# Splitting half of a weight matrix one group earlier, beside the first layer

## The chip, the cores and the metric

One core of a Trainium2 chip (trn2). The metric is device time of one execution, in microseconds (us). A ratio is the mean time of one kernel's fast runs over that of the other kernel's fast runs of the same rounds on the same chip, with a 95% interval, so it is not quite the ratio of the medians quoted beside it.

## The reference, cut to what matters

An attention with a decaying state (batch 4, 8 heads, 768 positions, width 48) gives a matrix x of 3072 rows and 384 columns. Four experts then work on all rows:

```python
p = domain_probs / (domain_probs.sum(-1, keepdims=True) + 1e-09)
for e in range(4):
    h = np.maximum(x @ w1[e], 0.0)          # w1[e]: 384 x 1024
    out += p[:, e:e + 1] * (h @ w2[e])      # w2[e]: 1024 x 384
```

Everything is float32, and the result has to be exact to that precision.

## The kernel before

The 3072 rows are 24 units of 128, in groups of 2, 4, 4, 4, 4, 4 and 2. For each group and expert the kernel runs the first layer (eight hidden tiles, each 128 hidden values by up to 512 rows), then the second layer (for each unit eight products of 128 x 128 by 128 x 384, one per hidden tile). Pieces of the next group's attention are put between the products.

An exact product is made in one of two ways. Either both operands are whole fp32, or both are three rounded parts (top, low and dif, type fp32r), and the product is top x top plus low x low in one sum and dif x dif in a second sum. (dif is made of top and low, so dif x dif holds both mixed terms, top x low and low x top. The first sum is scaled by 1 + 1/4096, FINE, and what dif x dif has too much then cancels. So three products do the work of four.) Making the parts of a weight piece takes two passes on ScalarE and two on VectorE. Each piece is split once, used and stored to memory ("kept", 1152 KB), and later groups load it from there.

```python
split1 = lambda gi, e: gi > 0        # first layer in parts from the second group (gi = 1) on
split2 = lambda gi, e: gi > 1        # second layer in parts from the third group on
makes  = [lambda gi, e: gi == 0, lambda gi, e: gi == 1]   # where w1 and w2 are split
```

So in the second group w2 is loaded whole, used whole, and split beside the second layer. The weights are loaded when the first layer begins (pieces 0 and 1) and at its third tile (2 and 3), into the parts of the hidden tiles that whole hidden values do not use:

```python
def up(gi, e, fc, slots=None):                       # one hidden tile of the first layer
    # ... [cut]
    if fc in ((0, 2) if gi == 1 else (0,)) and begins and not split2(gi, e):
        for k in half: load_piece(1, (gi * E + e) * NQ + k, beside=True)
    # ... [cut: nine matmuls into "one" (6) and "two" (3)]
        nc.scalar.activation(out=t, in_=one, func=ACT.Copy, scale=FINE)
        if split2(gi, e):
            nc.vector.tensor_add(t, t, two)
            finish.append(hidden_parts(t, parts))    # ScalarE: top; VectorE: low, dif (two halves)
        else:
            nc.vector.tensor_add(whole, t, two)
            finish.append(rectified(whole))          # ScalarE alone

def split_piece(l, i):
    whole = wt[l][i]
    # ... [cut]
    nc.scalar.activation(out=top, in_=whole, func=ACT.Copy, scale=TRIM)
    yield
    nc.scalar.activation(out=dif, in_=whole, func=ACT.Copy, scale=TRIM * 4096)
    yield
    nc.vector.scalar_tensor_tensor(out=low, in0=whole, scalar=4096.0, in1=dif.bitcast(F32), ...)
    nc.vector.tensor_sub(dif, low.bitcast(F32), top.bitcast(F32))
    nc.gpsimd.dma_start(out=kept[l][i % (E * NQ)], in_=w.bitcast(F32))

def down(gi, e, slots, between):                     # second layer: slots = one unit, or two in parts
    if slots[0] == 0 and makes[1](gi, e):
        making.extend(split_piece(1, first + k) for k in range(NQ))      # NQ = 4 pieces
    # ... [cut]
    steps = [(part, i, fc) for parts, tiles in (kinds if halves_ else [((3,), range(FCH))])
             for part in parts for i in range(len(slots)) for fc in tiles]   # part 3: whole
    # ... [cut: one matmul per step, then add_up() of each finished sum on VectorE]
    # after the last units of an expert: next group's pieces
        for c in range(NQ):
            if c < NQ // 2 or gi == LAST: load_piece(1, first + NQ + c)
            else: late.append(first + NQ + c)        # loaded after a later w1 piece
```

## Time and profile before

The time is 1080.85 us, the median of 3 runs (1079.32 to 1081.3). The prediction below shows the profile lines that carry the argument. What matters of them and of the starts of each layer in the timeline of TensorE (PE) is this; a stretch runs from the first matmul of one layer to the first of the next:

| | before |
|---|---|
| PE busy in the whole span | 98% |
| second group: length, PE idle in it | 185.54, 0.39 us |
| second group, experts 0 to 3: first layer | 21.66, 21.22, 22.22, 22.14 us |
| second group, experts 0 to 3: second layer | 27.03, 24.38, 23.40, 23.48 us |
| third group, expert 0: first, second layer | 22.64, 19.43 us |

Read it from the last row up. The same second layer takes 19.4 us where both operands are in parts and 23.4 to 24.4 us where they are whole (27.0 for expert 0, between whose products more of the attention lies). PE hardly idles in either. So most of the difference is work of the products, and it can be saved wherever the parts are ready in time.

### The profile page before, as it was taken

The page shows a single profiled execution, that of the slowest core. Times are in us where ns is not written, and L with a number is a line of the kernel's source. Part 1 is how long each engine was busy: PE and PEld are TensorE (multiplying, and loading weights), DVE is VectorE, ACT ScalarE, POOL GpSimd, SP SyncE. Part 2 cuts the span into 40 slices and gives each one's busy share as a digit, 9 for nine tenths or more (in the row PEclk, how much of TensorE's full clock was granted, in tenths as well). Part 3 has the DMA queues.
Part 4 walks back from the last instruction along what each step waited for, and adds up shares of the span by engine and source line. Part 5 has one row for each costly group of instructions (what it writes and reads, how often), then busy time and mean ns, then how long its engine had stood idle before and what let it go on. Part 6 is the DMA issues. An engine that isn't in the chain of part 4 may idle for free.

```text
span 1079.8 us, 21595 instructions
## 1 busy us (share of the span) xinstructions
PE 1055.5 (98%) x8460; PEld 899.6 (83%) x8460; DVE 774.5 (72%) x1711; ACT 566.8 (52%) x1202; POOL 32.7 (3%) x71
## 2 busy tenths in 40 slices
PE   8889899999999999999999999999999999999998
PEld 8767677676777798898898998888989889898988
DVE  5588678656557878777877786986878866666565
ACT  5786766764747455536446445555564543323232
POOL 2000000000000100000000000000000000000000
PEclk9999899999999999999999999999999999999999
DMA  8597679886686968659568568595594643544440
GB/s 124 155 329 227 213 230 378 301 315 240 234 295 208 399 203 318 253 147 351 204 221 324 195 228 320 159 327 222 168 352 146 249 191 136 215 172 180 182 182 33
DMA packets 158838, 251.67 MB, mean 233 GB/s; under 512 B 120112, under 2 KB 135344, under 8 KB 136208
## 3 DMA queue, kind: packets, MB, share of 16 engines
q1 hardware_dynamic: 149600, 208.82, 56.2%
q0 software_dynamic: 5760, 41.29, 9.7%
q8 instruction: 67, 1.10, 0.4%
q10 hardware_dynamic: 3376, 0.17, 0.3%
q14 instruction: 35, 0.29, 0.1%
HBM read 207.79 MB, written 42.47 MB: 232 GB/s over the span
## 4 chain that ended last, share of the span: by engine, by line
PE 80%; DVE 8%; ACT 6%; issue 2%; SPq 2%; DMA 1%; ACTq 0%; DVEq 0%
PE ops L615 26%; PE one L531 21%; PE two L531 10%; PE ops L619 9%; PE sc L333 5%; PE yps L425 3%; PE tp L265 2%; ACT qb L307 2%; PE one L523 2%; PE sps L454 1%; DVE near L343 1%; DVE hT L571 1%; PE far L388 1%; DVE t L544 1%; SPq L211 1%
## 5 line engine op out<-in xcount | busy, mean ns | idle before, releaser
L615 PE MATMUL ops<-w,hT 128*128 128x384 f32 x1728 | 318.6, 340 | 2.8 <-DVE acc L649 2.8
L615 PEld LDWEIGHTS ops<-w,hT 128*128 128x128 f32 x1728 | 299.1, 188 | 8.2 <-DVE acc L649 4.1
L531 PE MATMUL one<-xT,w 128*128 128x512 f32 x960 | 253.7, 400 | 0.8 <-DMA w<-kept 0.5
L531 PEld LDWEIGHTS one<-xT,w 128*128 128x128 f32 x960 | 175.9, 188 | 42.0 <-issue 2.4
L542 ACT ACTIVATE t<-one 128x512 f32<-128x512 f32 (+1 forms) x192 | 106.5, 555 | 163.8 <-PE one L531 144.1
L307 ACT COPY qb<-QT 64x256 f32<-64x256 f32 x336 | 136.5, 406 | 72.0 <-DVE QT L288 34.8
L569 ACT ACTIVATE hT<-t 128x512 fp32r<-128x512 f32 (+1 forms) x160 | 94.3, 589 | 111.3 <-DVE t L544 110.1
L571 DVE SCALAR_TENSOR_TENSOR hT<-t,hT 128x512 fp32r<-128x512 f32 (+1 forms) x160 | 102.0, 638 | 60.5 <-ACT hT L569 58.8
L531 PE MATMUL two<-xT,w 128*128 128x512 f32 x480 | 136.3, 392 | 0.0
L619 PE MATMUL ops<-hT 128*128 128x384 f32 x384 | 135.8, 497 | 0.0
L544 DVE TENSOR_TENSOR t<-t,two 128x512 f32<-128x512 f32 (+1 forms) x160 | 100.8, 630 | 39.5 <-ACT t L542 21.1
L581 DVE SCALAR_TENSOR_TENSOR hT<-hT 128x256 fp32r<-128x256 f32 x288 | 112.0, 421 | 4.4
L531 PEld LDWEIGHTS two<-xT,w 128*128 128x128 f32 x480 | 90.2, 188 | 19.8
L619 PEld LDWEIGHTS ops<-hT 128*128 128x128 f32 x384 | 70.0, 192 | 40.5 <-issue 1.4
L343 DVE COPY_PREDICATED near<-masks,sc 128x256 f32<-128x256 uint8 x144 | 77.0, 535 | 18.0 <-PE sc L333 14.9
L314 DVE TENSOR_TENSOR QT<-QT,dec 128x256 f32<-128x256 f32 x144 | 60.7, 421 | 34.3 <-ACT qb L307 33.9
L333 PEld LDWEIGHTS sc<-qb,KT 128*64 128x64 f32 x2304 | 73.3, 139 | 9.2 <-issue 7.1
L333 PE MATMUL sc<-qb,KT 128*64 128x64 f32 x2304 | 77.6, 224 | 0.2 <-ACT qb L307 0.2
L649 DVE SCALAR_TENSOR_TENSOR acc<-ops,p_all,acc 128x384 f32<-128x384 f32 x82 | 49.4, 612 | 29.1 <-PE ops L615 14.2
L326 DVE TENSOR_TENSOR KT<-KT,dec 128x256 f32<-128x256 f32 x144 | 60.2, 418 | 2.8 <-PE tp L265 2.8
L325 ACT COPY KT<-KT 128x256 f32<-128x256 f32 x144 | 59.7, 415 | 3.1
L549 DVE TENSOR_TENSOR hT<-t,two 128x512 f32<-128x512 f32 x32 | 22.0, 688 | 35.5 <-ACT t L542 28.6
(88 smaller groups left out, 972.6 us busy)
## 6 DMA issues: line engine op xcount, KB each, us to landing
w<-kept SPq DMA_DIRECT2D x144, 1152.0 KB
kept<-w POOLq DMA_DIRECT2D x32, 1152.0 KB, 7.6
hT<-in_moe_w_dram SPq DMA_DIRECT2D x32, 384.0 KB
w<-in_moe_w_dram SPq DMA_DIRECT2D x48, 128.0 KB
ra<-in_alpha_dram SPq DMA_DIRECT2D x23, 192.0 KB
rk<-in_k_dram SPq DMA_DIRECT2D x23, 192.0 KB
rq<-in_q_dram SPq DMA_DIRECT2D x23, 192.0 KB
out_dram<-acc POOLq DMA_DIRECT2D x18, 192.0 KB, 6.4
```

The source lines that it names most:

```text
L307: nc.scalar.copy(out=qb[rows, :, i, :].rearrange("p a (b r) -> p a b r", r=m), in_=qv[rows])
L314: nc.vector.tensor_mul(qv, qv, spread(dv[:, :, :, 0], m))
L333: nc.tensor.matmul(out[HALF * s:HALF * (s + 1), 2 * p:2 * p + 2, :], lhsT=KTs[li][:, p, HALF * s:HALF * (s + 1)], rhs=qbs[li][:, p, :, QUA ...
L343: nc.vector.copy_predicated(near.rearrange("p a (b two r) -> p a b two r", two=2, r=m)[:, :, :, 1, :], mk.unsqueeze(1).broadcast_to([P, H, ...
L531: nc.tensor.matmul(out, lhsT=w[:, part, kc], rhs=x_part(gi, part, kc), start=(part == terms[0] and kc == 0), stop=(part == terms[-1] and k ...
L542: nc.scalar.activation(out=t, in_=one, func=ACT.Copy, scale=FINE)
L544: nc.vector.tensor_add(t, t, two)
L569: nc.scalar.activation(out=top, in_=x, func=ACT.Relu, scale=TRIM)
L571: nc.vector.scalar_tensor_tensor(out=low, in0=x, scalar=0.0, in1=top.bitcast(F32), op0=ALU.max, op1=ALU.subtract)
L581: nc.vector.scalar_tensor_tensor(out=dif, in0=top.bitcast(F32), scalar=1 / 4096.0, in1=low.bitcast(F32), op0=ALU.mult, op1=ALU.subtract)
L615: nc.tensor.matmul(sums[i][part // 2], lhsT=h[:, part], rhs=w, start=(fc == 0 and part != 1), stop=(fc == FCH - 1 and part != 0))
L619: nc.tensor.matmul(sums[i][0], lhsT=h[:, 2].bitcast(F32), rhs=w, start=(fc == 0), stop=(fc == FCH - 1))
```

## The change

The intent is to get a part of that saving one group earlier. For experts 1 to 3 of the second group, the first half of w2 (pieces 0 and 1, hidden tiles 0 to 3) is split beside the first layer, from its third tile on, and used in parts at once. The other half stays whole and is split beside the second layer as before. The first expert keeps the old form. The core of the diff:

```diff
-    split2 = lambda gi, e: gi > 1
+    split2 = lambda gi, e, c=0: gi > 1 or gi == 1 and e > 0 and c < NQ // 2
@@ load_piece: where the whole piece is put
-            w = hidden[c][:, 0].rearrange("p f n -> p (f n)")[:, :KC * QF].bitcast(F32)
+            place = (hidden[c][:, 0] if not split2(gi, e, c) else hidden[c + NQ // 2][:, 1])
+            w = place.rearrange("p f n -> p (f n)")[:, :KC * QF].bitcast(F32)
@@ split_piece
+        elif split2(1, *divmod(i - E * NQ, NQ)):
+            wt[1][i] = w
@@ up
+        if gi == 1 and e > 0 and fc in (2, 4):
+            making.append(split_piece(1, first_piece(gi, e) + fc // 2 - 1))
@@ down
-            making.extend(split_piece(1, first + k) for k in range(NQ))
+            making.extend(split_piece(1, first + k) for k in range(NQ // 2 if halves_ else 0, NQ))
+        elif gi == 1:
+            kinds = [((0, 1), range(FCH // 2)), ((3,), range(FCH // 2, FCH)), ((2,), range(FCH // 2))]
... [cut: starts and ends of sums worked out from the list of steps]
@@ cost, by which attention is dealt out between products
-        return 4.1 if split2(gi, e) else 5.4
+        return 4.1 if gi > 1 else 4.7 if split2(gi, e) else 5.4
```

More of the change, by code (lines that the diff above doesn't have):

```diff
@@ L190, in load_piece @@
         e, c = divmod(k, NQ)
-        if (split1, split2)[l](gi, e):
+        if gi > l:
             w = wt[l][i] = wts.tile([P, 3, KC * QF], F32R, name=f"w{l + 1}",
@@ L502, in up @@
                 hidden[k] = hid.tile([P, 3, FPQ, NT], F32R, name="hT", bufs=NQ)
-        if fc in ((0, 2) if gi == 1 else (0,)) and begins and not split2(gi, e):
+        if fc in ((0, 2) if gi == 1 else (0,)) and begins and gi < 2:
             half = range(fc, fc + 2) if gi == 1 else range(NQ)
@@ L542, in up @@
             nc.scalar.activation(out=t, in_=one, func=ACT.Copy, scale=FINE)
-            if split2(gi, e):
+            if split2(gi, e, c):
                 nc.vector.tensor_add(t, t, two)
@@ L600, in down @@
         kinds = [((0, 1), range(FCH - 2)), ((0, 1), range(FCH - 2, FCH)), ((2,), range(FCH))]
-        steps = [(part, i, fc) for parts, tiles in (kinds if halves_ else [((3,), range(FCH))])
+        if not halves_:
+            kinds = [((3,), range(FCH))]
+        elif gi == 1:
+            kinds = [((0, 1), range(FCH // 2)), ((3,), range(FCH // 2, FCH)), ((2,), range(FCH // 2))]
+        steps = [(part, i, fc) for parts, tiles in kinds
                  for part in parts for i in range(len(slots)) for fc in tiles]
+        sides = [[s for s, step in enumerate(steps) if (step[0] // 2 if halves_ else 0, step[1]) == key]
+                 for key in ((side, i) for i in range(len(slots)) for side in range(len(sums[0])))]
+        firsts, lasts = {s[0] for s in sides}, {s[-1] for s in sides}
         for n, (part, i, fc) in enumerate(steps):
@@ L605, in down @@
             h = hidden[c][:, :, f, slots[i] * P:(slots[i] + 1) * P]
-            advance(cost(1, gi, e) / FCH / (3 if halves_ else 1))
+            advance(cost(1, gi, e) * len(slots) / len(steps))
             while between and n >= between[0][0] * len(steps):
@@ L612, in down @@
                 make_dif(*later.popleft())
-            if halves_:
+            side = part // 2 if halves_ else 0
+            if part < 3:
                 w = wt[1][first + c].rearrange("p t (c d) -> p t c d", d=DM)[:, part, f]
-                nc.tensor.matmul(sums[i][part // 2], lhsT=h[:, part], rhs=w,
-                                 start=(fc == 0 and part != 1), stop=(fc == FCH - 1 and part != 0))
+                h = h[:, part]
             else:
                 w = wt[1][first + c].rearrange("p (c d) -> p c d", d=DM)[:, f]
-                nc.tensor.matmul(sums[i][0], lhsT=h[:, 2].bitcast(F32), rhs=w,
-                                 start=(fc == 0), stop=(fc == FCH - 1))
-            if part >= 1 and fc == FCH - 1:
-                add_up(gi, e, slots[i], part // 2, sums[i][part // 2 if halves_ else 0])
+                h = h[:, 2].bitcast(F32)
+            nc.tensor.matmul(sums[i][side], lhsT=h, rhs=w, start=(n in firsts), stop=(n in lasts))
+            if n in lasts:
+                add_up(gi, e, slots[i], part // 2, sums[i][side])
         while between:
```

## The prediction

In its second block of profile lines two of four rows are printed: the rows that its text calls the second and the fourth are the first and the second there.

> **What bounds the kernel now.** I read the page first (busy shares, the forty slices, the chain that ended last), then tables of busy time by stretch, then the matmuls in order of time, because this change touches one stage only and its worth has to be read there.
>
> ```profile
> PE 1055.5 (98%) x8460; PEld 899.6 (83%) x8460; DVE 774.5 (72%) x1711; ACT 566.8 (52%) x1202; POOL 32.7 (3%) x71
> PE 80%; DVE 8%; ACT 6%; issue 2%; SPq 2%; DMA 1%; ACTq 0%; DVEq 0%
> L619 PE MATMUL ops<-hT 128*128 128x384 f32 x384 | 135.8, 497 | 0.0
> ```
>
> TensorE is busy 98% of the span and makes 80% of the chain. The third line is the work that the change aims at: second-layer products on whole fp32 operands, 384 records. The two groups that use them make 2 units x 4 experts x 8 tiles = 64 and 4 x 4 x 8 = 128 products, 192 in all, so each whole product is two records.
>
> Next, the stage. The second group runs from 172.86 us (its first first-layer matmul) to 358.4 us (the third group's first). The second row below is that group, the fourth all later groups of four units together. The columns are length, then busy time and count of PE, PEld, DVE, ACT and POOL, then the clock, the DMA share and GB/s.
>
> ```profile
> 172.86:358.40 185.54, 185.15 (x1325) 132.62 (x1325) 118.76 (x241) 115.56 (x230) 8.52 (x16) 1.00 0.80 277
> 358.40:880.00 521.60, 517.79 (x4457) 460.15 (x4456) 414.96 (x936) 271.17 (x574) 9.12 (x17) 1.00 0.69 250
> ```
>
> PE idles for 0.39 us of 185.54 in the second group, so time taken from TensorE there comes off the end, unless a new wait takes its place. VectorE is at 64% there and ScalarE at 62%.
>
> What one product costs is read from starts in the timeline of PE (start, length, line, count), since the lengths of neighbours overlap:
>
> ```profile
> 208.28 4.04 PE L619 MATMUL ops<-hT 128*128 128x384 f32 x12
> 212.16 0.60 PE L265 MATMUL tp<-ident,rk 128*128 128x128 f32 x4
> ...
> 391.86 8.77 PE L615 MATMUL ops<-w,hT 128*128 128x384 f32 x49
> 400.46 1.54 PE L531 MATMUL one<-xT,w 128*128 128x512 f32 x6
> ```
>
> Twelve whole records take 212.16 - 208.28 = 3.88 us, 323 ns each, so a whole product is 647 ns. Forty-nine part records (line 615, the third group) take 8.60 us, 175.5 ns each; other blocks give 176 to 179, and I use 176. Three of them make one exact product: 528 ns.
>
> **What the Trainium skill says.** "FP8 and Floating Point Precision", section "TensorE Precision Notes", gives true FP32 four passes through the array. "TensorE: Matmul & The Clock Gate", section "Back-to-back issue gap", gives about N/2.4 + 2.5 ns for one pass, 162.5 ns at N = 384. The trace agrees for whole products: 647 = 4 x 161.7. It does not for the parts: 176 ns instead of 162, so three passes for four do not save a full pass of 162 ns. The same page's section "LDWEIGHTS (loading the stationary operand)" gives 128/1.2 = 107 ns for a load of 128 columns; here line 615 has 1728 loads of 188 ns mean, longer than the 176 ns gap itself, which may be why the gap is not 162 (no run shows that yet). The same page's table of specifications calls ScalarE and VectorE strict FIFOs. That matters for the first rival: a split that waits for its weights holds every eviction behind it.
>
> **The change part by part.** It concerns experts 1 to 3 of the second group (4 units each) and pieces 0 and 1 of 4, which are hidden tiles 0 to 3 of 8.
>
> TensorE: 3 experts x 4 units x 4 tiles = 48 whole products become parts. Removed 48 x 647 = 31.0 us, added 144 x 176 = 25.3 us: 5.7 us off the engine that sets the end. The other half stays whole. First-layer and attention matmuls keep their number; attention is only dealt a little earlier.
>
> VectorE: tiles 0 to 3 now need top, low and dif. The addition before costs the same in both places (0.69 against 0.68 us), and the ScalarE pass too (0.63 both). New are one low of 0.692 us and two dif halves of 0.421 us per tile: 12 tiles x 1.53 = 18.4 us. Two sums per unit in place of one add 12 accumulations of 0.61 us: 7.4 us. Together 25.8 us, which takes VectorE to about 144.5 of 180 us, 80%: what the later groups run at now (414.96/521.60 = 80%). Nothing of this lies on the path by itself.
>
> Splits: the same 16 pieces, each two ScalarE passes of 0.84 us and two VectorE passes of 0.95 us, and the same stores. For pieces 0 and 1 of three experts they move from beside the second layer to beside the first: 3.4 us of ScalarE and 3.8 us of VectorE per expert. First-layer stretches of experts 1 to 3 now, and of the third group's first expert:
>
> ```profile
> 221.50:242.80 21.30, 21.30 (x199) 17.39 (x197) 10.86 (x24) 16.84 (x36) 0.00 (x0) 1.00 0.86 310
> 267.10:289.40 22.30, 22.30 (x207) 18.26 (x206) 10.59 (x22) 13.90 (x28) 0.00 (x0) 1.00 0.76 276
> 312.80:334.90 22.10, 22.10 (x206) 18.09 (x204) 10.95 (x24) 13.33 (x28) 0.00 (x0) 1.00 0.94 309
> 358.40:381.00 22.60, 22.60 (x210) 18.50 (x208) 19.88 (x42) 13.12 (x26) 2.66 (x5) 1.00 1.01 415
> ```
>
> VectorE there goes from about 10.8 to 10.8 + 4 x (0.692 + 0.421) + 3.8 = 19.1 us of 22, as in the fourth row, where PE never idles at 19.88. ScalarE goes to 20.2 of 21.3 us for expert 1 and about 17 of 22 for the others. In the second-layer stretches VectorE loses 3.8 us of splits and gains 4 x 0.42 + 4 x 0.61 = 4.1: no change.
>
> Waits that this brings: I add 1.2 us. The later groups, which already work in this way at this VectorE load, have PE idle 521.60 - 517.79 = 3.8 us in 521.6, that is 0.73%, or 1.3 us in 180, against 0.39 now: +0.9. Walking ScalarE's queue for expert 1 (copy 0.59, rectify 0.63, the splits, and the attention copies in their new order) has one group of attention scores waiting about 0.5 to 1 us for a copy that came behind a split; I take a third of a microsecond of that beyond the average.
>
> Sum: 1080.85 - 5.7 + 1.2 = 1076.3 us.
>
> **The rivals.** First, ScalarE is held up by weights that have not landed. Until now the whole w2 had the whole first layer to arrive; now the first pass over piece 0 stands in ScalarE's queue right after tile 2, some 7 us after the first layer begins, and everything behind it (copies out of PSUM, attention's copies) would wait with it. Its new place in a hidden tile of the other half also comes free later, because those tiles are read last: about 2.7 us later for expert 1. For the rival: the issues of these loads stand only a few microseconds before the stage, and DMA is busy.
>
> ```profile
> 217.56 2.45 SPq L214 DMA_DIRECT2D hT<-in_moe_w_dram  x2
> 263.80 2.12 SPq L214 DMA_DIRECT2D hT<-in_moe_w_dram  x2
> 309.43 2.02 SPq L214 DMA_DIRECT2D hT<-in_moe_w_dram  x2
> ```
>
> "DMA: Bandwidth & Descriptors", section "Issuing engines are not separate DMA queues", says that transfers from all queues run on the same 16 engines and interleave; the packets in the trace agree, for the two loads of 217.56 move at about 222 to 227 us beside a store of split weights and behind a load of queries. Against the rival: ScalarE needs piece 0 only at about 228.7 us, and after the change only two stores per expert are left at that point for experts 2 and 3. If it bites, PE loses 1 to 3 us per expert: 1078 to 1083 us.
>
> Second, parts run at 162 ns, if what lengthens them in the later groups is absent here. The saving is 48 x (647 - 487) = 7.7 us and the time about 1073.5. All blocks of line 615 that I looked at are at 175 to 179, even those with little else running, so I give it little.
>
> Third, sums or DMA become the bound. Four sums are open at once in four PSUM buffers; in the third to sixth groups line 615 waited 6.9 us in 8 cases for an accumulation on VectorE, which is in my average already; double that is 1077.5. The third group's first w2 pieces now can only be loaded once the last products have read the split weights, some 7 us closer to their use, in a stretch where DMA is at 1.01. In the kernel before they are ready at least 3 us early, and the reserve at the new place is some 4 us by my count; a miss would add 1 to 3 us.
>
> **Range and chances.** The saving of 5.7 us has an error of about 0.5 from the gap; the waits may be 0 to 6 us; the runs of before spread over 2 us (1079.32 to 1081.3). That gives 1073.5 to 1079.8. A gain of 2% would need 21.6 us, nearly four times what is taken from TensorE; a loss of 2% would need waits of 27 us, over 9 per expert. I give each 1%.
>
> **What would show it.** Right: 288 whole records left of 384 and 1872 part records instead of 1728; the second group (first first-layer matmul to the next group's) about 181 us long instead of 185.5, with PE idle there under 2 us; VectorE near 145 us in it; the rest of the span as before. The first rival would show as gaps of PE in the first layer of experts 1 to 3, ended by ScalarE, with ScalarE's pass over the whole weights ended by a DMA; the third as gaps before line 615's successor, ended by the accumulation or a DMA of kept weights. I am wrong if the stage shortens by less than 2 us or by more than 7, or if the time moves outside the second group.

## The result, and the profile after

The changed kernel takes 1074.95 us, the median of 4 runs (1073.09 to 1076.09), against 1080.8 us for the kernel before in the same rounds (4 runs, 1079.32 to 1081.3). The ratio is 0.9947 [0.9929, 0.9964]. This is "same" at a margin of 2%, and a real gain of half a per cent. The result is correct. The prediction of 1076.3 us was 1.35 us too high and its range holds the result.

First the page of the changed kernel: the busy shares, the chain that ended last, and the second layer's two groups of products. The line numbers have moved: both forms are now issued from line 633.

```profile
PE 1048.4 (98%) x8508; PEld 905.8 (84%) x8508; DVE 795.8 (74%) x1759; ACT 565.9 (53%) x1202; POOL 32.8 (3%) x71
PE 82%; DVE 8%; ACT 6%; issue 2%; DMA 2%; SPq 0%; ACTq 0%; DVEq 0%
...
L633 PE MATMUL ops<-w,hT 128*128 128x384 f32 x1872 | 349.9, 341 | 2.7 <-DVE acc L662 2.7
L633 PE MATMUL ops<-hT 128*128 128x384 f32 x288 | 102.8, 499 | 0.0
```

There are 288 whole records and 1872 part records, as predicted: 96 whole records went and 144 part records came. PE stays at 98%, so the kernel is still bound by the same engine.

Next the busy times by stretch: the second group, then all groups between it and the end that have four units. The columns are as in the prediction.

```profile
172.74:352.37 179.63, 179.27 (x1372) 139.93 (x1373) 137.88 (x286) 113.04 (x225) 8.12 (x16) 1.00 0.80 276
352.37:874.00 521.63, 517.87 (x4456) 460.31 (x4456) 415.90 (x939) 272.85 (x579) 9.53 (x18) 1.00 0.70 253
```

The group takes 179.63 us instead of 185.54: 5.91 us less. Ahead of it the time is 172.74 against 172.86 us, and the four groups after it take 521.63 against 521.60 us. All of the gain is in the stage that was changed. PE idles for 0.36 us there, against 0.39 before.

Not all of these 5.91 us are the change, though. About 0.5 us of them lie in the first layer of expert 0, which the change does not touch (21.13 us instead of 21.66). Later runs with the same code there took from 20.87 us (quarter) to 21.67 us (dealt), according to whether a wait for inputs fell before or after the first matmul of the group. Experts 1 to 3 take 131.47 us (the six stretches below) instead of 136.84 (the table above), 5.37 us less. Another 0.29 us shows just behind them, where the first six matmuls of the third group take 1.40 us (352.37 to 353.77) instead of 1.69 (358.39 to 360.08). So the 48 products saved 5.4 to 5.7 us, 112 to 118 ns each.

Within the stage, the second-layer stretches of experts 1 to 3 before, then after:

```profile
242.80:267.10 24.30, 24.30 (x125) 15.48 (x124) 17.64 (x35) 11.86 (x23) 2.12 (x4) 1.00 0.65 219
289.40:312.80 23.40, 23.40 (x119) 14.56 (x117) 17.48 (x35) 13.76 (x26) 2.12 (x4) 1.00 0.72 230
334.90:358.40 23.50, 23.50 (x121) 14.65 (x117) 19.19 (x37) 16.02 (x32) 1.59 (x3) 1.00 0.69 233
```

```profile
243.06:264.90 21.84, 21.84 (x134) 17.16 (x134) 16.71 (x39) 9.59 (x20) 0.53 (x1) 1.00 0.65 187
286.87:308.65 21.78, 21.78 (x133) 17.08 (x132) 14.55 (x34) 11.19 (x23) 1.06 (x2) 1.00 0.65 199
330.49:352.37 21.88, 21.88 (x136) 17.22 (x133) 20.28 (x45) 11.95 (x26) 0.66 (x2) 1.00 0.47 164
```

In every row the second number (PE busy) equals the first (length): PE has no gap, before or after, and the rows are shorter because there is less to do. (Expert 1's row also loses 0.8 us of attention matmuls that now stand in its first layer, at 242.25 us.) The first-layer stretches of the same experts after the change show where the splits went:

```profile
220.90:243.06 22.16, 22.16 (x207) 18.14 (x205) 15.90 (x30) 18.00 (x35) 1.06 (x2) 1.00 0.95 359
264.90:286.87 21.97, 21.97 (x205) 18.07 (x205) 19.46 (x36) 16.63 (x32) 1.06 (x2) 1.00 0.96 349
308.65:330.49 21.84, 21.84 (x206) 17.97 (x205) 18.59 (x36) 14.56 (x29) 1.06 (x2) 1.00 0.92 330
```

VectorE (the fourth number, counts in brackets left out) rose from 10.6 to 11.0 us to between 15.9 and 19.5 us. For the last two experts that is close to the 19.1 us of the prediction. PE does not idle here either. The change is carried by engines that had the time.

The cost of one product, from starts in the timeline of PE of the changed kernel:

```profile
286.87 2.99 PE L633 MATMUL ops<-w,hT 128*128 128x384 f32 x16
289.70 5.32 PE L633 MATMUL ops<-hT 128*128 128x384 f32 x16
...
294.86 0.60 PE L268 MATMUL tp<-ident,ra 128*128 128x128 f32 x4
```

Sixteen part records take 289.70 - 286.87 = 2.83 us, 177 ns each. Sixteen whole records take 5.16 us, 322.5 ns each. With 112 to 118 ns saved per product, a part record costs (647 - 112) / 3 = 178 to (647 - 118) / 3 = 176 ns on average, which agrees. The expectations below use 122.5 ns per product (5.88 us of PE's busy time over 48), which counts the half microsecond of expert 0 too.

### The profile page after: what moved, and what is told of

It reads as the page before. It is cut to its first block, busy times and chain, and to the rows that moved or that the text cites. A ratio compares the mean times of both kernels' runs of the same rounds, so it can differ in the third digit from the quotient of the medians.

```text
span 1073.6 us, 21720 instructions
## 1 busy us (share of the span) xinstructions
PE 1048.4 (98%) x8508; PEld 905.8 (84%) x8508; DVE 795.8 (74%) x1759; ACT 565.9 (53%) x1202; POOL 32.8 (3%) x71
## 4 chain that ended last, share of the span: by engine, by line
PE 82%; DVE 8%; ACT 6%; issue 2%; DMA 2%; SPq 0%; ACTq 0%; DVEq 0%
PE ops L633 35%; PE one L536 21%; PE two L536 10%; PE sc L336 5%; PE yps L428 3%; PE tp L268 3%; ACT qb L310 2%; PE one L528 2%; PE sps L457 1%; DVE hT L576 1%; PE far L391 1%; DVE t L549 1%; DVE near L346 1%; DMA w<-kept 1%; ACT hT L574 1%
## 5 line engine op out<-in xcount | busy, mean ns | idle before, releaser
L633 PE MATMUL ops<-w,hT 128*128 128x384 f32 x1872 | 349.9, 341 | 2.7 <-DVE acc L662 2.7
L633 PEld LDWEIGHTS ops<-w,hT 128*128 128x128 f32 x1872 | 324.1, 188 | 10.0 <-DVE acc L662 4.0
L574 ACT ACTIVATE hT<-t 128x512 fp32r<-128x512 f32 (+1 forms) x172 | 101.8, 592 | 118.2 <-DVE t L549 116.7
L576 DVE SCALAR_TENSOR_TENSOR hT<-t,hT 128x512 fp32r<-128x512 f32 (+1 forms) x172 | 110.4, 642 | 66.3 <-ACT hT L574 64.4
L549 DVE TENSOR_TENSOR t<-t,two 128x512 f32<-128x512 f32 (+1 forms) x172 | 109.0, 634 | 42.1 <-ACT t L547 21.8
L586 DVE SCALAR_TENSOR_TENSOR hT<-hT 128x256 fp32r<-128x256 f32 x312 | 122.0, 422 | 4.8
L633 PE MATMUL ops<-hT 128*128 128x384 f32 x288 | 102.8, 499 | 0.0
L633 PEld LDWEIGHTS ops<-hT 128*128 128x128 f32 x288 | 52.9, 193 | 29.9 <-issue 1.6
L662 DVE SCALAR_TENSOR_TENSOR acc<-ops,p_fine,acc 128x384 f32<-128x384 f32 x60 | 35.8, 612 | 21.8 <-PE ops L633 21.7
```

The costliest lines, as they stand in the source:

```text
L574: nc.scalar.activation(out=top, in_=x, func=ACT.Relu, scale=TRIM)
L576: nc.vector.scalar_tensor_tensor(out=low, in0=x, scalar=0.0, in1=top.bitcast(F32), op0=ALU.max, op1=ALU.subtract)
L586: nc.vector.scalar_tensor_tensor(out=dif, in0=top.bitcast(F32), scalar=1 / 4096.0, in1=low.bitcast(F32), op0=ALU.mult, op1=ALU.subtract)
L633: nc.tensor.matmul(sums[i][side], lhsT=h, rhs=w, start=(n in firsts), stop=(n in lasts))
L662: nc.vector.scalar_tensor_tensor(out=acc, in0=part, scalar=scale, in1=acc, op0=ALU.mult, op1=ALU.add)
```

## The experiments

The kernel before ran beside each group of experiments: 1079.68 us median with the first four, 1079.97 with the next four, 1080.26 with the last two. There are two theories about the result. The **main theory** says that the gain is PE's saved work and nothing else, and that it comes in full as long as every feeder (ScalarE, VectorE, DMA) has some reserve left. The **rivals** say that one of these feeders already takes part of the gain, or that the size of the gain has another cause (the dealing of attention). The experiments push each reserve until it breaks.

| run | median us (lowest to highest) | ratio to before |
|---|---|---|
| again | 1074.19 (1073.32 to 1074.67) | 0.9942 [0.9929, 0.9954] |
| quarter | 1079.87 (1078.53 to 1081.87) | 0.9998 [0.9985, 1.0012] |
| quarterswap | 1077.62 (1076.11 to 1077.96) | 0.9971 [0.9957, 0.9986] |
| three | 1078.51 (1078.09 to 1079.64) | 0.9988 [0.9976, 1.0001] |
| early | 1079.09 (1077.98 to 1080.05) | 0.9992 [0.9978, 1.0006] |
| first | 1082.25 (1081.02 to 1085.01) | 1.0025 [1.0009, 1.0041] |
| firstlateswap | 1076.42 (1075.52 to 1079.14) | 0.9966 [0.995, 0.9981] |
| moredif | 1075.44 (1074.5 to 1076.14) | 0.9953 [0.9939, 0.9967] |
| dealt | 1074.75 (1074.29 to 1076.84) | 0.9956 [0.9943, 0.9969] |
| narrow (wrong result on purpose) | 1021.91, one run, state unknown | none |

One run of the kernel before, in the last group, took 3671.15 us. It counts as slow and is in no ratio.

### again: the changed kernel once more

No edit. It serves as the reference for the second group of runs.

> The changed kernel unaltered, on the chip and in the rounds of the runs beside it, as their common measure. It should be 5.5 to 6 us below the kernel before: about 1074 if that is at 1079.7 here.

It measured 1074.19 us and repeats the first result.

### quarter: one piece instead of two

```diff
-    split2 = lambda gi, e, c=0: gi > 1 or gi == 1 and e > 0 and c < NQ // 2
+    split2 = lambda gi, e, c=0: gi > 1 or gi == 1 and e > 0 and c < NQ // 4
-        if gi == 1 and e > 0 and fc in (2, 4):
+        if gi == 1 and e > 0 and fc in (2,):
     # and NQ // 2, FCH // 2 become NQ // 4, FCH // 4 in the place, the splits and the steps
```

> Only piece 0 (hidden tiles 0 and 1) is split early and used in parts, by the same experts 1 to 3: 24 whole products become parts instead of 48. If the gain is the shorter TensorE work alone, 24 x 122.5 ns (what the changed kernel saved per product: 5.88 us over 48) = 2.9 us, so about 1077.9 us beside 1080.8 before and 1074.95 with half. If part of the gain came from elsewhere (the earlier dealing of attention, or units taken in pairs), more than half of it is kept: 1076 or less.

It measured 1079.87 us: no gain that can be told from none. Yet the second group did get shorter. The third group starts at 355.56 us, against 358.39 in the kernel before. That is 2.83 us, but 0.8 of it is expert 0's first layer again. Experts 1 to 3 take 134.72 us instead of 136.84: 2.1 us saved, where 24 products of 112 to 118 ns make 2.7 to 2.8. Of what is missing, some 0.4 us lie in expert 3's first layer (22.27 us instead of 21.84 in the changed kernel, with a wait of 0.16 us). The larger loss comes afterwards, in the second layer of the third group's first expert. It takes 23.83 us, where the changed kernel takes 19.92. Its timeline of PE, then its row of busy times:

```profile
381.02 5.45 PE L633 MATMUL ops<-w,hT 128*128 128x384 f32 x21 [2.19 <-DMA w<-kept]
```

```profile
377.53:401.36 23.83, 21.64 (x150) 20.89 (x148) 15.36 (x40) 10.41 (x25) 0.00 (x0) 0.93 0.79 264
```

PE stands still for 2.19 us until a piece of w2 has landed from the kept copies. The first 21 records after it take 5.29 us, 252 ns each instead of about 177, and the mean granted clock of the row is 0.93. Why is the piece late? The queue of GpSimd (POOL), which issues the stores of split pieces, shows it for the changed kernel and then for this one, at the end of the second group:

```profile
352.25 0.53 POOL L231 DMA_DIRECT2D kept<-w  x1 [19.48 <-DVE QT L317]
356.16 0.53 POOL L231 DMA_DIRECT2D kept<-w  x1 [3.38 <-ACT KT L328]
```

```profile
354.89 0.53 POOL L231 DMA_DIRECT2D kept<-w  x1 [24.88 <-DVE QT L317]
358.94 0.53 POOL L231 DMA_DIRECT2D kept<-w  x1 [3.52 <-ACT KT L328]
360.80 0.53 POOL L231 DMA_DIRECT2D kept<-w  x1 [1.33 <-ACT lat L408]
```

With one piece split early, three remain to be split beside the second layer, and three stores of 1152 KB instead of two are issued, from 0.7 us before the third group begins to 5.2 us after, just when its weights are to be loaded. That is the prediction's third rival, in a kernel where it bites. The number of stores alone does not explain it: the kernel before issues four there and does not wait, but the first two come 12.4 and 9.0 us before its third group (at 345.95 and 349.42 us). That the third store is what makes the piece late is read from these times; the next run tests the order of the loads behind it.

### quarterswap: the same, with the order of two loads turned round

```diff
     # on top of quarter, in up(), before the next w1 piece is loaded:
+            while late and (gi, e) == (2, 0):
+                load_piece(1, late.popleft())
```

The third and fourth w2 pieces of the third group are asked for ahead of a w1 piece instead of behind it. No work is taken away.

> The version with one piece saved 2.8 us by the start of the third group and then lost them: 2.19 us of TensorE waiting for a DMA of kept w2 parts in that group's first second layer, with the clock at 0.93 after it. Here the third and fourth piece of that expert are asked for before the next expert's w1 piece instead of after it; nothing else differs. If the order of the transfers is the cause, the wait goes and the gain of the 24 shorter products is back: about 2.9 us below the kernel before. If the pieces are late because their stores to memory land late, they stay late, and the time stays that of the kernel before.

It measured 1077.62 us. The stretch that had taken 23.83 us takes 19.93, and PE does not wait for w2 in it. What came back is 2.25 us by medians of two groups of rounds, or 2.9 by the ratios. The gain over the kernel before is 2.35 us by medians, or 3.1 us by the ratio (1.5 to 4.6 by its interval), where 24 products make 2.7 to 2.8. So the order of the transfers causes the wait, and the saving of half as many products fits the same figure, within a wide interval.

### three: three pieces instead of two

```diff
-    split2 = lambda gi, e, c=0: gi > 1 or gi == 1 and e > 0 and c < NQ // 2
+    split2 = lambda gi, e, c=0: gi > 1 or gi == 1 and e > 0 and c < NQ - 1
+        if gi == 1 and e > 0 and fc == 6:
+            load_piece(1, first_piece(gi, e) + 3, beside=True)     # the whole piece comes late
-        if gi == 1 and e > 0 and fc in (2, 4):
-            making.append(split_piece(1, first_piece(gi, e) + fc // 2 - 1))
+        if gi == 1 and e > 0 and fc in (2, 3, 4):
+            making.append(split_piece(1, first_piece(gi, e) + fc - 2))
     # the places of the whole pieces and the ranges of the steps follow
```

> Three of four pieces in parts, only the last whole (loaded late, into the place of piece 1 once that is split): 72 products become parts. TensorE alone: 72 x 122.5 ns = 8.8 us, 1072.0 us. Rival: VectorE. It was busy 19.5 of 21.97 us in expert 2's first layer; 2 more tiles of low and dif (2 x 1.11 us) and one more split (1.9 us) make 23.6 of 22, so TensorE would wait about 1.5 us per expert there, and the time would be about 1074 to 1076, no better than with half.

It measured 1078.51 us, 3.6 us worse than the changed kernel by medians of different rounds (4.4 by the ratios), although 24 more products became cheaper. The second group of this kernel, and what PE waited for in it (us in total, times, longest):

```profile
171.32:355.01 183.69, 178.46 (x1397) 142.68 (x1398) 144.34 (x300) 112.26 (x225) 8.55 (x16) 1.00 0.80 276
```

```profile
PE ops L635 <- DVE hT L556: 2.8, 2, 1.6
PE one L538 <- DMA w<-kept: 1.6, 1, 1.6
PE ops L635 <- DVE acc L664: 0.9, 2, 0.6
PE two L538 <- DVE t L551: 0.7, 1, 0.7
PE ops L635 <- ACT hT L592: 0.6, 1, 0.6
```

PE idles 183.69 - 178.46 = 5.23 us. The second line is the idle time just ahead of the first matmul, which ends where the group begins; the other four sum to 5.0 us, nearly all of it. The largest wait, of second-layer products, is for an addition on VectorE (line 556, which makes a tile that stays whole), and three of these four lines, 4.4 us, are VectorE's. So here PE does wait for VectorE, at 144.34 of 183.69 us busy, which is 79% in the mean. A mean below 80% says little: in the second-layer stretches of experts 1 to 3, where all of these waits but the 0.7 us lie, it was busy 20.44, 19.56 and 21.91 us of 22.11, 23.70 and 22.77. But its load alone is not the cause either: moredif, further down, has the same busy time in all, and 20.71 of 21.89 us in expert 3's second layer, and PE does not wait there. The difference may be what stands ahead of the addition in VectorE's queue; no run tests that. Another thing stays open: 24 products should have taken some 2.8 us off PE's busy time, and it fell by 0.81 only (178.46 against 179.27).

### early: the two splits two tiles earlier

```diff
-        if gi == 1 and e > 0 and fc in (2, 4):
-            making.append(split_piece(1, first_piece(gi, e) + fc // 2 - 1))
+        if gi == 1 and e > 0 and fc in (0, 2):
+            making.append(split_piece(1, first_piece(gi, e) + fc // 2))
```

> The splits begin at tiles 0 and 2 instead of 2 and 4; nothing else differs. ScalarE then asks for the whole w2 piece 0 some 4 us earlier, before its packets have moved (in the changed kernel they end at about 227.4 us for expert 1, and ScalarE began its pass over it at 227.72). The first rival of the prediction, were it given the chance: ScalarE waits for a DMA, and with two tiles' reserve in PSUM TensorE waits for 0 to 3 us per expert: 1075 to 1082 us. If the reserve swallows it, 1075 with ScalarE's pass shown waiting for a DMA and no gap on PE.

It measured 1079.09 us, and the loss is where the first rival said: the first layers of experts 1 and 2 take 25.95 and 23.72 us instead of 22.16 and 21.97. Its timeline of ScalarE (ACT), then of PE:

```profile
226.18 0.84 ACT L224 ACTIVATE w<-hT 128x768 fp32r<-128x768 f32 x1 [3.25 <-DMA hT<-in_moe_w_dram]
```

```profile
228.87 1.75 PE L536 MATMUL one<-xT,w 128*128 128x512 f32 x6 [1.76 <-ACT t L547]
230.42 1.48 PE L536 MATMUL two<-xT,w 128*128 128x512 f32 x3
231.81 2.50 PE L536 MATMUL one<-xT,w 128*128 128x512 f32 x6
```

ScalarE waits 3.25 us for the whole piece. The copy out of PSUM behind it waits too, and so PE waits 1.76 us for that copy. Then comes a second price. The last line's six records take 2.50 us, where six such records take 1.54 in the changed kernel. The granted clock is still 1.00 from 228.8 to 230 us, with PE at work again; from 230 to 233.5 us it is 0.54. Of the 3.79 us lost in this stretch 1.76 are the wait; the clock after it makes 3.5 x 0.46 = 1.6 of the rest.

This run also measures the reserve. The piece had landed by 226.18 us, 5.73 us after the layer began (at 220.45). In the changed kernel, where the layer begins at 220.90 us, ScalarE reaches the same instruction at 227.72, after 6.82 us:

```profile
227.72 0.84 ACT L224 ACTIVATE w<-hT 128x768 fp32r<-128x768 f32 x1
```

So the third tile is right by a margin of about 1.1 us for expert 1, if the piece lands as long after the layer's start in both. (The 227.4 us of the expectation is where the packets of both pieces, 0 and 1, end.) For expert 3 the earlier split cost nothing (21.83 against 21.84 us), so the margin is not the same everywhere.

### first: the first expert too

```diff
-    split2 = lambda gi, e, c=0: gi > 1 or gi == 1 and e > 0 and c < NQ // 2
+    split2 = lambda gi, e, c=0: gi > 1 or gi == 1 and c < NQ // 2
-        if gi == 1 and e > 0 and fc in (2, 4):
+        if gi == 1 and fc in (2, 4):
```

> The first expert of the second group is treated as the other three: 16 more products in parts, 16 x 122.5 ns = 2.0 us less on TensorE: 1073.0 us if nothing waits. Rival: at the start of the group DMA has no room (share 1.03 in the first layer of expert 0 before the change, two short waits for weights there already), so ScalarE waits for the whole w2 with evictions behind it: 1075 to 1080 us. I expect the rival.

It measured 1082.25 us, slower than the kernel before. The first layer of the first expert takes 27.91 us instead of 21.13. ScalarE (ACT) in its timeline:

```profile
185.00 0.84 ACT L224 ACTIVATE w<-hT 128x768 fp32r<-128x768 f32 x1 [5.75 <-DMA hT<-in_moe_w_dram]
```

The chain is the same as in early, and longer: 5.75 us on ScalarE, then 3.37 us on PE for the copy behind it (at 188.09 us), and six records in 2.93 us after that. From 188 to 195 us the clock is 0.55. It shows what the change avoids by leaving the first expert out.

### firstlateswap: the first expert with late splits

```diff
     # on top of first:
-        if gi == 1 and fc in (2, 4):
-            making.append(split_piece(1, first_piece(gi, e) + fc // 2 - 1))
+        if gi == 1 and fc in ((2, 4) if e else (5, 6)):
+            making.append(split_piece(1, first_piece(gi, e) + (fc // 2 - 1 if e else fc - 5)))
     # the splits are finished at the last tile, and the loads are ordered as in quarterswap
```

> A try at a faster version: the first expert of the group takes part too, but its splits begin at tiles 5 and 6, after the moment at which its whole w2 landed when it was tried from tile 2 on (13.9 us after the group's start, ScalarE waiting 5.75 us, TensorE 3.4), and the transfers at the start of the third group are swapped as in the run beside this. If ScalarE's wait was all that cost: 16 products x 122.5 ns = 2.0 us below the changed kernel. If the other three waits of the first try (on VectorE and ScalarE near 171, 203 and 238 us, 3.6 us) are still there, it is 1 to 2 us above the changed kernel.

It measured 1076.42 us. Splitting late takes away the long wait, but short ones remain on PE: 0.54 us for a split (at 195.34 us), 0.90 and 1.32 us for copies of the attention (at 199.55 and 233.81 us). With 16 more products there were 1.8 to 1.9 us to be had, and the kernel is 2.2 us slower than the changed one in the same rounds. I found no version that beats the changed kernel.

### moredif: more work for VectorE, nothing else

```diff
-                finish.append(hidden_parts(t, parts))
+                finish.append(hidden_parts(t, parts, 2 if gi == 1 else 1))   # every dif made twice
```

> The changed kernel with every dif of the second group's hidden tiles computed twice (the same values again): 24 more VectorE instructions of 0.42 us, 10.1 us, half in the first layers and half in the second. If VectorE at 77% (137.9 of 179.6 us) has reserve, as the absent waits say, nothing or less than 1 us is lost. If it was at its limit, as with three pieces, where TensorE waited 5.2 us of 183.7, 3 to 6 us are lost.

The second group has 24 more VectorE instructions, some 10 us of work (its dif records take 20.0 us instead of 9.9), and the same result.

```profile
171.56:351.39 179.83, 179.59 (x1373) 139.84 (x1373) 144.25 (x306) 112.76 (x225) 8.00 (x15) 1.00 0.80 275
```

VectorE's busy time rises by 6.4 us to 144.25 (busy time counts overlapping records once), as high as in three, and the group takes 179.83 us with PE idle for 0.24. So VectorE is not what sets the time of the changed kernel in this stage, and it has room there. The whole kernel took 1075.44 us, 1.25 us more than again by medians, with overlapping intervals of the ratios. About one us of it is the third group's first layer (23.05 us instead of 22.07), outside the stage; I did not follow that further.

### narrow: part products of 256 columns instead of 384

```diff
-            nc.tensor.matmul(sums[i][side], lhsT=h, rhs=w, start=(n in firsts), stop=(n in lasts))
+            into = sums[i][side]
+            if part < 3 and n not in firsts and n not in lasts:
+                into, w = into[:, :256], w[:, :256]
+            nc.tensor.matmul(into, lhsT=h, rhs=w, start=(n in firsts), stop=(n in lasts))
```

This leaves a third of most sums out, so the result is wrong (relative error 0.49). The loads of weights stay the same. If the load, recorded at 188 ns, sets the spacing of part products, it stays near 175 ns; if streaming sets it, the spacing falls. The 122 ns of the expectation are an estimate: 256 columns at the 2.4 columns per ns of the formula that the prediction quotes, and 15 ns more.

> Wrong result on purpose, from the changed kernel: in all groups the second-layer part products that neither begin nor end a sum take 256 columns instead of 384; their weight loads stay as they are (128 columns, 188 ns). Asked is what makes a part record take 175 ns from start to start[...]. If a fixed cost of about 15 ns per record is added to the streaming, the gap of the narrow ones falls to [...]122 ns. If the weight load sets it, the gap stays near 175 ns.

A stretch of its timeline of PE, at full clock:

```profile
538.78 3.93 PE L636 MATMUL ops<-w,hT 128*128 128x256 f32 x29
542.55 1.55 PE L536 MATMUL one<-xT,w 128*128 128x512 f32 x6
```

Twenty-nine records take 542.55 - 538.78 = 3.77 us, 130 ns each; another stretch, from 418.75 us on, has 43 in 5.40 us, 125.6 ns each. A few of them keep 384 columns. The spacing follows the columns and falls well below 188 ns, so the recorded length of a weight load does not set it. The first layer's records in the same traces agree: nine of 512 columns take 2.06 us (229 ns each), nine of 256 take 1.08 us (120 ns each). Taken at 2.4 columns per ns, as in the formula that the prediction quotes, streaming would be 107, 160 and 213 ns for 256, 384 and 512 columns. An fp32r record takes 13 to 18 ns more at each of the three widths (120, 176 to 178 and 229 ns). What these 13 to 18 ns are stays open.

### dealt: the old cost in the dealing of attention

```diff
-        return 4.1 if gi > 1 else 4.7 if split2(gi, e) else 5.4
+        return 4.1 if gi > 1 else 5.4
```

> The changed kernel with the old figure (5.4 instead of 4.7) for the second layer of the second group in the model that deals out attention; so attention stands in the order of work as if the stage were as long as before. If the gain is the shorter products alone, the time stays within 1 us of the changed kernel (1074.2 in the last rounds). If the earlier dealing is part of why no new waits came, 1 to 3 us are lost.

It measured 1074.75 us. The attention is dealt differently (expert 1's first and second layer take 19.04 and 26.40 us instead of 22.16 and 21.84), and one wait of PE of 1.2 us for an attention copy appears. Against again the intervals of the ratios overlap. The gain does not come from the dealing; whether the new figure is worth nothing or up to about 1.5 us is not settled.

## Why the prediction was right

It was right in its mechanism and nearly in its size. By its own steps:

**The saving on TensorE was right.** It said 48 products, 119 ns each, 5.7 us. Measured are 5.4 to 5.7 us in the three experts that changed, 112 to 118 ns each; the 5.91 us of the whole stage hold 0.5 us of expert 0 besides. The counts came out to the record. The half-sized version fits the same figure once its late transfer is removed (quarterswap).

**The added waits were the mis-sized term.** It said +1.2 us: 0.9 from the idle share of the later groups and 0.3 from a score waiting behind a split. Measured is none: PE idles 0.36 us in the group, against 0.39. These 1.2 us are most of the 1.35 us by which the point was off. That the whole was so close is in part luck, since single runs of one kernel spread over 2 to 3 us. The later groups' idle share was not a property of their VectorE load: moredif raises VectorE to the same load in this stage and PE idles for 0.24 us.

**VectorE's work was right in number and too high as busy time.** It said 118.76 + 25.8 = 144.5 us; measured are 137.88, so 19.1 instead of 25.8. The group has 45 more VectorE records where the working counts 48. It multiplied counts by recorded lengths, but records of neighbours overlap, and busy time counts an overlap once. Summed over the trace, the lengths rose by 23.4 us (129.6 to 152.9), so overlap makes about 4 of the 6.7 us, and records fewer than counted most of the rest. In the timeline of VectorE (DVE) of the changed kernel the second record starts before the first, by its length, has ended:

```profile
225.65 0.42 DVE L586 SCALAR_TENSOR_TENSOR hT<-hT 128x256 fp32r<-128x256 f32 x1
225.99 0.68 DVE L549 TENSOR_TENSOR t<-t,two 128x512 f32<-128x512 f32 x1
```

It is the prediction's own rule for PE (take starts, not lengths), not applied to VectorE.

**The first rival did not bite, by about 1.1 us.** Its chain (DMA, ScalarE, everything behind it, PE) was described rightly: early and first show it link by link. What the prediction missed is its second price, the clock after the gap, which doubled the loss in early.

**The second rival did not come.** Parts stayed at 176 to 178 ns. The guess given for that, that the weight load of 188 ns is the cause, is refuted by narrow.

**The third rival did not bite either, but its reserve was probably put too high.** It said "some 4 us" for the next group's w2 pieces. Quarter, with one more store in their way, missed by 2.19 us. An estimate, if that store is all that differs: 1152 KB at the 378 GB/s that were moved in the changed kernel from 352.37 to 374.45 us are 3.1 us, and 3.1 - 2.2 leaves a reserve of about 1 us. No run measures it directly. For the sums it quoted 6.9 us of waits in 8 cases in the later groups. That figure appears to add PE's own wait, which the kernel before shows as follows, to 4.1 us that the weight loads waited for the same accumulations at the same time:

```profile
PE ops L615 <- DVE acc L649: 2.8, 4, 1.2
```

PE's own is 2.8 us in 4 cases, and it could not have been 6.9 in groups in which PE idles for 3.8 us altogether. After the change it is 2.7 us.

## What to carry to other kernels

Where PE had no gaps, a cheaper form of a product brought its saved PE time here, and no more than that; count products, take the cost of each from differences of starts, and multiply. Then ask for every feeder by how many microseconds it is early, because that margin, not its busy share, decides whether the gain arrives: here about 1 us on one load, and by an estimate as little on another, carried it, and going one tile earlier, one expert further or one piece more or less gave it all or much of it back. A wait of 2 us on PE can cost about 4, since the clock may fall for a few microseconds after it (3.8 us lost around 1.76 in early, 3.9 around 2.19 in quarter). It need not: again idles for 1.73 us just before its second group, three for 1.59 at 335.14 us, and the clock stays at 1.00 in the microseconds after both.

## What the Trainium skill lacked or had wrong

- "TensorE: Matmul & The Clock Gate", section "What's actually happening", ties the half clock to an idle window of about 3.4 us. Here shorter gaps were enough: after 1.76 us of idle PE (early) the clock was 0.54 from 230 to 233.5 us, and after 2.19 us (quarter) 21 records ran at 252 ns instead of about 177. After 3.37 us (first) it was 0.55 for 7 us. Length alone does not decide, for after 1.73 us (again) and 1.59 us (three) it stayed at 1.00.
- The same page, section "Back-to-back issue gap", gives N/2.4 + 2.5 ns, and less, about 131 ns at N = 512, in a sustained stream. Products of fp32r parts follow neither here: about 120, 177 and 229 ns at 256, 384 and 512 columns, that is 13 to 18 ns above the streaming time at 2.4 columns per ns. Whole fp32 products do follow it (647 ns for four passes).
- The same page, section "LDWEIGHTS (loading the stationary operand)", gives 107 ns for 128 columns. The records here are 188 ns long, yet part products of 256 columns follow each other at 126 to 130 ns, so the recorded length is not a spacing.
- "FP8 and Floating Point Precision", section "TensorE Precision Notes", gives the four passes of fp32. No page gives the price of the other way to an exact product, three rounded parts: about 530 ns instead of 647 at 384 columns, plus the splitting and a second sum on VectorE.
